# Steps 5 to 45 of a segment recurrence: K and V row chunks shared by both feature halves, two more head blocks of Wo paired, and another filler table

## The chip, the cores and the metric

The kernel runs on one core of a Trainium2 chip. The metric is the device time of one execution in microseconds, as the median of several runs. A NeuronCore has the engines PE (TensorE: matmuls, and PEld, its weight loads), DVE (VectorE), ACT (ScalarE), POOL (GpSimd) and SP (SyncE, which here issues DMAs). They run side by side and wait for one another by semaphores.

## The reference, cut to what matters

A layer of segment-recurrent attention with a memory of 8 rows, followed by a gated feed-forward layer. `x` is (1, 2048, 640), H = 32 heads of 128, segments of 32 rows, 64 segments one after the other:

```python
for s in range(n_seg):                       # 64 steps
    h = concat([mem, xs], axis=1)            # 8 memory rows + 32 rows of x
    q, k, v = h @ Wq, h @ Wk, h @ Wv         # 640 -> 32 heads x 128
    p = softmax(mask(q @ k.T * scale))
    o = (p @ v) @ Wo                         # 4096 -> 640
    mem = o[:, :M]                           # the next step's memory
    outs.append(o[:, M:])
h  = x + attention(layernorm(x))
h2 = h + ffn(layernorm(h))
```

The next step's memory rows are this step's output, so the 64 steps can't run side by side.

## The kernel before, in words

All operations are put into one list by a Python class. Each names its engine and the tiles and PSUM banks that it reads and writes, and the class derives the waits between engines; each engine then runs its own operations in the order of the list. So the order of the Python calls is the order on each engine.

A step handles 32 rows at once: 8 rows of memory and 24 of x. The last 8 rows of each segment are done for four segments together, in passes that the steps run as extra work (`extra_units`, called by `filler`). An activation tile has 128 rows by 32 columns and is the stationary operand of a matmul; the weights W are streamed past it, 512 columns at a time. Four such matmuls go side by side in the four column groups of the array (g = 0 to 3). One such set of four is called a round here, and its four weight loads a round of loads.

`project` (L398) computes one of K (j = 1), Q (j = 0) or V (j = 2) for a feature half (i = 0 or 1, 2048 features each) from five row chunks c of 128 rows, added up in one PSUM bank: five rounds for each half, so 30 rounds a step for K, Q and V. Half 0 of K and V goes to bank P2, half 1 to P3; Q uses P0 and P1. Every round loads its chunk of the activation. `held=True` leaves out the first load, where the same chunk was used just before (`again`, L390, a matmul without a load; `WAYS` runs half 1 through the chunks backwards so that this fits). `parts` cuts a 512-column matmul into two of 256, each with a load of its own.

The table `FILL` and `fill_of` say for each step how many such extra instructions are put in: loads that could have been held, and split matmuls. With them four steps issue 3072 PE instructions.

A step's order on PE, by the calls in the loop: K (half 0 in chunks 0 to 2, which need only the first part of the new memory, key "m"; then chunks 3 and 4, key "m2"; then half 1), the previous step's value product (`pv_x`, L712), Q, V half 0 in chunks 0 to 3, scores of half 0 (`scores`, L515) in two parts around chunk 4, V half 1 in the same way around the scores of half 1, the memory rows' products (`pv_mem`, L569) with `filler` work between them, and Wo.

After each half of K and Q, ACT copies the bank to SBUF (`to_tok`, L443) and DVE transposes it (`flip`, L438). The halves of V are copied by ACT alone (`to_v`, L443, tile Vp). `pv_mem(s, 0)` needs Vp's half 0 and the masked exponents Pbd from DVE.

Wo is done in two passes, each over 16 head blocks. `wo_split` (L634) takes eight pairs of head blocks, with 320 columns and four matmuls to a pair, into bank P1. `wo_pass` (L617) takes the other 16 blocks one by one, with 160 columns and four matmuls to a block, into P3. `fold_split` folds P1 to the sum SA: two DVE transposes (L647), two ACT copies (L650), and one addition, on POOL in three of four steps and on DVE in the steps with s % 4 = 1 (L652). `to_act_split` transposes P3 on DVE (L661) and adds SA (L663) into the next step's activation, in two parts (m and m2). `rows_split` then reads P3 (L668) and P1 (L670) for the output rows. Extra work (`filler(2)`) stands on PE between Wo and the next step's K.

Of the kernel before, what the change touches and what calls it, by code (L numbers as in the profile page):

```python
# [27 lines left out]
class _Graph:  # L28
# [149 lines left out]
def build_kernel(nc, A_x, A_mem0, A_Wq, A_Wk, A_Wv, A_Wo, A_seg_len, B_W_gate, B_W_up, B_W_down, out):  # L178
    _, S, D = A_x.shape
    M = A_mem0.shape[1]  # L180
    _, H, Dh = A_Wq.shape
# [97 lines left out]
    def bank(b):  # L279
        return ps[:, b * 512:(b + 1) * 512]  # L280
# [19 lines left out]
    def B(n):  # L300
        return ("B", n)
# [96 lines left out]
    def project(act, akeys, j, halves, banks, chunks=range(5), ends=(0, DC - 1), held=False, parts=0):  # L398
        swap = 1 if j == 2 and akeys[0][0] == "acte" else 0

        def f(pe):
            left = parts
            for c in chunks:
                for n, i in enumerate(halves):
                    for g in range(4):
                        o = 2048 * i
                        w = (W[:, j, c, o + 512 * (g ^ swap):o + 512 * (g ^ swap) + 512] if j == 2 else
                             W[:, j, c, o:o + 2048].rearrange("p (h e) -> p h e", e=128)[:, :, 32 * g:32 * g + 32])
                        a = (bank(banks[n])[32 * g:32 * g + 32, :], act[:, c, :], w)
                        if n == 0 and not (held and c == chunks[0]):  # L410
                            k = min(left, 2) if c != ends[0] else 0
                            left -= k
                            for q in range(2 if k else 1):
                                b = a if not k else (a[0][:, 256 * q:256 * q + 256], a[1],
                                                     w[:, 256 * q:256 * q + 256] if j == 2 else w[:, 8 * q:8 * q + 8])
                                if q and k == 1:
                                    ins = again(pe, *b, c == ends[0], c == ends[1], g)
                                else:
                                    ins = pe.matmul(*b, start=(c == ends[0]), stop=(c == ends[1]), skip_group_check=True)  # L419
# [181 lines left out]
    def oT_keys(p, hf):  # L601
        return [("oT", p, n, hf) for n in "mx"]
# [3 lines left out]
        add("pool", lambda g: g.tensor_copy(oTe[:, :, o:o + M], oT[p][:, :, 32:40]),  # L606
            r=[("oT", p, "x", kh) for kh in range(2)], w=[("oTe", s % 4)])

    def wo_pass(p, bk, halves=(0, 1), groups=range(4)):
        src = oT[p]  # L610
        for hf in halves:
            for lo, hi in [(4 * g, 4 * g + 4) for g in groups]:
                def f(pe, hf=hf, lo=lo, hi=hi):
                    for hb in CH[16 * hf + lo:16 * hf + hi]:
                        w = Wo[:, hb, :].rearrange("p (c g j) -> p g c j", g=4, j=32)
                        for gg in range(4):
                            i = pe.matmul(bank(bk)[32 * gg:32 * gg + 32, 0:160], src[:, hb, 0:32], w[:, gg],  # L617
                                          start=(hb == CH[16 * halves[0]]), stop=(hb == CH[-1]), skip_group_check=True)
                    return i
                add("pe", f, r=oT_keys(p, hf) + [("Wo", hf, lo // 4)], w=[B(bk)])  # L620

    def wo_split(p, bk):
        for g in range(4):
            wo_pairs(p, bk, g)

    def wo_pairs(p, bk, group):
        src = oT[p]

        def f(pe):
            for n in (2 * group, 2 * group + 1):  # L630
                for q in range(4):
                    hb = CH[2 * n + q // 2]
                    w = ap(Wo, hb * D + 32 * q, [[64 - 128 * (q // 2), 2], [128, DC], [1, 32]])
                    i = pe.matmul(bank(bk)[32 * q:32 * q + 32, 0:320], src[:, hb, 0:32], w, start=(n == 0),  # L634
                                  stop=(n == 7), skip_group_check=True)
# [525 lines left out]
    row_moments(xl, ("xl",), n_rows(1))  # L1161

    WAYS = ((range(DC), (0, DC - 1)), (range(DC - 1, -1, -1), (DC - 1, 0)))
    FILL = (56, 39, 7, 52)

    def fill_of(s):
        n = {1: 0, 2: 0, 3: 0, 4: 27, 52: 40, 56: 40, 50: 0, 51: 25, 54: 0, 55: 25, 57: 39, 58: 0, 59: 27, 60: 40, 61: 39, 62: 50, 63: 0}.get(s, FILL[s % 4])
        alone = min(n // 4, 3)
        rest = n - 4 * alone
        return [k < 3 - alone for k in range(3)], [2 * ((rest // 2 + k) // 4) + (k == 0 and rest % 2) for k in range(4)]  # L1170

    for s in range(1, NSEG):
        last = s == NSEG - 1
        par = s % 2
        nb = s // 4 + 1
        ln = 64 + 128 * nb < S
# [12 lines left out]
        if s > 0:  # L1189
# [19 lines left out]
                    dma(farv_d[:, 512 * i:512 * i + 512], tok[2 + i], r=tok_keys(2 + i), w=[("farv", i)])  # L1209
                dma(ends_d[:, :], ends[:, :], r=END_KEYS, w=[("ends",)])  # L1210
            for i in range(2):
                if i == 0:
                    soon = min(parts[0], 8 * (KC - 1))
                    project(a, [k for k in ks if k[-1] != "m2"], 1, (0,), (P2,), range(KC), parts=soon)
                    project(a, ks, 1, (0,), (P2,), range(KC, DC), parts=parts[0] - soon)
                else:
                    project(a, ks, 1, (1,), (P3,), *WAYS[1], held=held[0], parts=parts[1])
                to_tok((P2, P3)[i], i, "act")
                if last and i == 1:
                    load_piece(("Ko", 0), "act")  # L1220
                flip(i, Ko, i, [("Ko", i)])
# [36 lines left out]
            if last:  # L1258
                load_piece(("Vp", 0), "act")
# [13 lines left out]
        if last:  # L1273
# [303 lines left out]
```

## Time and profile before

| | us |
|---|---|
| median of 3 runs | 976.83 (975.82 to 977.68) |
| the profiled execution, its own time | 977.37 |
| its span, first to last instruction | 975.4 |
| granted TensorE clock, mean | 1.00 |

How to read what follows: L12 is line 12 of the kernel. A line of the timeline gives the start in us from the span's start, the duration in us, the engine, the source line, the operation, what it writes and reads, the shape and a count of instructions merged into the line, and in brackets the engine's idle time just before with what ended it ("issue" where the profile shows nothing waited for). Starts of PE are the measure of its pace; the duration of a matmul runs from its start to its modelled end and overlaps with the next one's.

### The profile page before, as it was taken

Reading aid. Unit: us, or ns where it says so; the run is one execution under the profiler, and the core shown is the slowest. Engines: PE = TensorE matmul, PEld = TensorE weight load, DVE = VectorE, ACT = ScalarE, POOL = GpSimd, SP = SyncE. Lnnn points to the kernel's source line nnn. Section 1 sums busy time; section 2 is a strip of 40 time slices with the busy share of each in tenths; the row PEclk is TensorE's granted clock in tenths of the full one; section 3 lists DMA queues with packets and bytes.
Section 4 is the critical chain, followed back from the end, with each engine's and each line's share of the span. In section 5 each row is a group of like instructions: output and inputs, shape, how many; then the busy total and the mean of one; then the engine's idle time right before and its main releaser. Section 6 shows DMA issues by size and latency. Waiting matters only on the chain.

```text
span 975.4 us, 56715 instructions
## 1 busy us (share of the span) xinstructions
PE 952.1 (98%) x26144; PEld 536.0 (55%) x24915; DVE 726.6 (74%) x2041; ACT 522.6 (54%) x1326; POOL 185.7 (19%) x423
## 2 busy tenths in 40 slices
PE   4999999999999999999999999999999999999998
PEld 1345565655665656565656565566666665444444
DVE  3668888888888888888888888888888883445332
ACT  1476666666666666666666666655555552122121
POOL 7021212121313131313131313020201110000000
PEclk9999999999999999999999999999999999999999
DMA  9961212222232323232323322232424246714100
GB/s 363 416 229 47 44 47 43 55 52 56 59 80 61 76 61 76 64 77 66 79 62 78 65 63 55 43 96 71 128 74 117 69 125 212 278 21 95 28 14 28
DMA packets 97300, 91.95 MB, mean 94 GB/s; under 512 B 57674, under 2 KB 80658, under 8 KB 94994
## 3 DMA queue, kind: packets, MB, share of 16 engines
q1 hardware_dynamic: 95328, 87.36, 31.5%
q8 instruction: 201, 3.29, 1.4%
q10 hardware_dynamic: 1730, 0.96, 0.4%
q14 instruction: 41, 0.34, 0.1%
HBM read 50.75 MB, written 15.22 MB: 68 GB/s over the span
## 4 chain that ended last, share of the span: by engine, by line
PE 94%; SPq 3%; DMA 2%; issue 1%; POOL 0%; ACT 0%; DVE 0%; POOLq 0%
PE ps L419 47%; PE ps L1066 9%; PE ps L617 7%; PE ps L392 7%; PE ps L634 7%; PE ps L683 4%; PE ps L1390 3%; PE ps L918 3%; SPq L357 3%; PE ps L515 3%; PE ps L712 2%; DMA Wo<-in_A_Wo_dram 2%; PE ps L569 1%; PE ps L1079 0%; PE ps L1405 0%
## 5 line engine op out<-in xcount | busy, mean ns | idle before, releaser
L419 PE MATMUL ps<-W,act_r 128*32 128x512 bf16 (+1 forms) x8335 | 466.4, 360 | 0.6 <-ACT tok L443 0.4
L419 PEld LDWEIGHTS ps<-W,act_r 128*32 128x32 bf16 x8335 | 218.9, 96 | 166.0 <-issue 22.4
L443 ACT ACTIVATE tok<-ps 128x512 bf16<-128x512 f32 x184 | 106.3, 594 | 60.9 <-PE ps L419 48.1
L443 ACT ACTIVATE tox<-ps 128x512 bf16<-128x512 f32 x138 | 81.8, 598 | 59.3 <-PE ps L419 48.9
L438 DVE STREAM_TRANSPOSE Ko<-tox 128x512 bf16<-128x512 bf16 x128 | 89.0, 696 | 29.3 <-ACT tox L443 28.6
L419 PE MATMUL ps<-W,act_e 128*32 128x512 bf16 x1008 | 97.3, 383 | 3.5 <-DVE TBf L496 2.0
L597 DVE STREAM_TRANSPOSE oT<-tox 128x512 bf16<-128x512 bf16 x128 | 94.8, 741 | 0.0
L438 DVE STREAM_TRANSPOSE Qo<-tok 128x512 bf16<-128x512 bf16 x124 | 85.5, 689 | 0.9 <-ACT tok L443 0.2
L617 PE MATMUL ps<-Wo,oT 128*32 128x160 bf16 x4032 | 82.0, 233 | 1.2 <-DMA Wo<-in_A_Wo_dram 1.0
L634 PE MATMUL ps<-Wo,oT 128*32 128x320 bf16 x2016 | 80.0, 299 | 0.4 <-DVE oT L591 0.4
L617 PEld LDWEIGHTS ps<-Wo,oT 128*32 128x32 bf16 x4032 | 70.5, 97 | 11.7 <-DVE oT L591 2.7
L443 ACT ACTIVATE Vp<-ps 128x512 bf16<-128x512 f32 x127 | 75.2, 592 | 0.5 <-ACT Vp L443 0.5
L392 PE MATMUL ps<-W,act_e 128*32 128x512 bf16 x712 | 70.5, 385 | 0.0
L1094 ACT ACTIVATE g<-ps 128x512 bf16<-128x512 f32 x43 | 25.0, 593 | 77.1 <-PE ps L1066 75.6
L650 ACT ACTIVATE SA<-TA 64x40 f32<-64x40 f32 x126 | 29.6, 235 | 65.3 <-DVE TA L647 64.5
L531 ACT ACTIVATE Pm<-ps 128x64 bf16<-128x64 f32 x126 | 28.1, 223 | 67.3 <-PE ps L515 66.1
L591 DVE STREAM_TRANSPOSE oT<-om 128x128 bf16<-128x128 bf16 x126 | 39.2, 311 | 31.1 <-ACT om L583 31.0
L515 PE MATMUL ps<-Qo,Ko 128*32 128x40 bf16 x2048 | 61.5, 181 | 0.0
L634 PEld LDWEIGHTS ps<-Wo,oT 128*32 128x32 bf16 x2016 | 51.1, 96 | 18.0 <-DVE rm L581 0.8
L515 PEld LDWEIGHTS ps<-Qo,Ko 128*32 128x32 bf16 x2048 | 46.8, 94 | 25.2 <-DVE Qo L438 17.7
L1095 DVE TENSOR_TENSOR hT<-g,ps 128x512 bf16<-128x512 bf16 x43 | 29.6, 688 | 40.1 <-PE ps L1066 35.5
L523 POOL COPY Qo<-ends 128x256 bf16<-128x256 bf16 x32 | 14.0, 438 | 238.2 <-DVE oT L591 231.2
(155 smaller groups left out, 1532.0 us busy)
## 6 DMA issues: line engine op xcount, KB each, us to landing
VM<-Vp SPq DMA_DIRECT2D x126, 65.0 KB
VM<-Vp SPq DMA_DIRECT2D x63, 130.0 KB
W<-in_A_Wk_dram SPq DMA_DIRECT2D x5, 1024.0 KB
W<-in_A_Wq_dram SPq DMA_DIRECT2D x5, 1024.0 KB
W<-in_A_Wv_dram SPq DMA_DIRECT2D x5, 1024.0 KB
Wo<-in_A_Wo_dram SPq DMA_DIRECT2D x8, 640.0 KB
attn_d<-wtok SPq DMA_DIRECT2D x248, 7.5 KB
xt<-in_A_x_dram SPq DMA_DIRECT2D x16, 160.0 KB
```

The source lines that it names most:

```text
L392: return pe.add_instruction(mybir.InstMatmult(name=nc.get_next_instruction_name(), engine=mybir.EngineType.PE, ins=[pe.lower_ap(rhs), pe.l ...
L419: ins = pe.matmul(*b, start=(c == ends[0]), stop=(c == ends[1]), skip_group_check=True)
L438: add("dve", lambda v: v.transpose(dst[:, 16 * i:16 * i + 16, 0:32], tok[t][:, :].rearrange("p (h f) -> p h f", f=32)), r=tok_keys(t), w=keys)
L443: add("act", lambda a: a.activation(dst, src, ACTF.Copy), r=r, w=w)
L515: i = pe.matmul(bank((P0, P1)[hf])[q:q + 32, o:o + 40], (Ko if a == 0 else Ke[p])[:, h, :], Qo[:, h, :], start=True, stop=True, skip_group ...
L591: add("dve", lambda v: v.transpose(ap(oT[par], 160 * hf, [[40, 4], [320, 4], [1, 8]]), ap(om, 128 * hf, [[1, 4], [4, 32]])), r=[("om", hf) ...
L597: add("dve", lambda v, kh=kh: v.transpose(ap(oT[p], 160 * kh + M, [[320, 4], [40, 4], [1, 32]]), ap(tox, 128 * kh, [[256, 4], [1, 4], [4, ...
L617: i = pe.matmul(bank(bk)[32 * gg:32 * gg + 32, 0:160], src[:, hb, 0:32], w[:, gg], start=(hb == CH[16 * halves[0]]), stop=(hb == CH[-1]), ...
L634: i = pe.matmul(bank(bk)[32 * q:32 * q + 32, 0:320], src[:, hb, 0:32], w, start=(n == 0), stop=(n == 7), skip_group_check=True)
L650: add("act", lambda a, lo=lo, to=to: a.activation(SA[to:to + 64], TA[lo:lo + 64, 1, :, 0:M], ACTF.Copy), r=[("TA", 1)], w=[("SA", to)])
L683: ins = pe.matmul(bank(bk)[32 * q:32 * q + 32, 0:320], src[:, hb, 0:32], w[:, 2 * (q % 2):2 * (q % 2) + 2], start=(i == 0), stop=(i == 15) ...
L1066: ins = pe.matmul(bank(bk), w[:, c, lo:lo + 128], xn2T[par][:, c, :], start=(c == 0), stop=(c == DC - 1))
```

## The change

`rounds` is new. It issues single rounds for a list of (chunk, half) pairs and loads a chunk only where it differs from the pair before, so that two neighbouring rounds on the same chunk, one for each half, share their loads. In steps 5 to 45 (`woven`):

- K runs as (0,0) (1,0) (2,0), (2,1), (3,0) (3,1) (4,0), then the copy of half 0, then (4,1) (1,1) (0,1). Half 1 begins at the fourth round, with the first keys ("m") alone.
- V runs as (0,0) (0,1) (1,0) (1,1), the scores around chunk 4 of half 0, then (2,0) (3,0), which end half 0 at chunk 3, then (3,1) (2,1), and the scores of half 1 around chunk 4 of half 1. ACT's copy of half 0 stays where it was in ACT's order, behind the exponent of the first scores.
- In steps with s % 4 other than 1, `wo_split` takes a ninth pair, the first two blocks of the second pass, and `wo_pass` skips them. The ninth pair needs the second half of oT.
- `FILL` becomes (0, 0, 2, 0); steps 3 and 4 get 60 filler instructions each; steps 46, 47 and 49 keep their old numbers by name, and step 48 gets 50 for 56.

```diff
+    def rounds(act, akeys, j, seq, ends, held=False):
+
+        def f(pe):
+            before = seq[0][0] if held else None
+            for c, i in seq:
+                for g in range(4):
+                    o = 2048 * i
+                    w = (W[:, j, c, o + 512 * g:o + 512 * g + 512] if j == 2 else
+                         W[:, j, c, o:o + 2048].rearrange("p (h e) -> p h e", e=128)[:, :, 32 * g:32 * g + 32])
+                    a = (bank((P2, P3)[i])[32 * g:32 * g + 32, :], act[:, c, :], w)
+                    start, stop = c == ends[i][0], c == ends[i][1]
+                    if c == before:
+                        ins = again(pe, *a, start, stop, g)
+                    else:
+                        ins = pe.matmul(*a, start=start, stop=stop, skip_group_check=True)
+                before = c
+            return ins
+        add("pe", f, r=list(akeys) + [("W", j, c) for c, _ in seq], w=[B((P2, P3)[i]) for i in sorted({i for _, i in seq})] + [("Wdone", j)])
+
...
-    def wo_pass(p, bk, halves=(0, 1), groups=range(4)):
+    def wo_pass(p, bk, halves=(0, 1), groups=range(4), skip=0):
...
-            for lo, hi in [(4 * g, 4 * g + 4) for g in groups]:
+            for lo, hi in [(max(4 * g, skip), 4 * g + 4) for g in groups]:
...
-    def wo_split(p, bk):
-        for g in range(4):
-            wo_pairs(p, bk, g)
-
-    def wo_pairs(p, bk, group):
+    def wo_split(p, bk, more=False):
+        for g in range(4 + more):
+            wo_pairs(p, bk, g, 7 + more)
+
+    def wo_pairs(p, bk, group, end=7):
...
-        add("pe", f, r=oT_keys(p, 0) + [("Wo", 0, group)], w=[B(bk)])
+        add("pe", f, r=oT_keys(p, group // 4) + [("Wo", group // 4, group % 4)], w=[B(bk)])
...
-    FILL = (56, 39, 7, 52)
+    FILL = (0, 0, 2, 0)
...
-        n = {1: 0, 2: 0, 3: 0, 4: 27, 52: 40, 56: 40, 50: 0, 51: 25, 54: 0, 55: 25, 57: 39, 58: 0, 59: 27, 60: 40, 61: 39, 62: 50, 63: 0}.get(s, FILL[s % 4])
+        n = {1: 0, 2: 0, 3: 60, 4: 60, 46: 7, 47: 52, 48: 50, 49: 39, 50: 0, 51: 25, 52: 40, 53: 39, 54: 0, 55: 25, 56: 40, 57: 39, 58: 0, 59: 27, 60: 40, 61: 39, 62: 50, 63: 0}.get(s, FILL[s % 4])
...
+        woven = 4 < s < 46
...
-                if i == 0:
+                if woven:
+                    first = [k for k in ks if k[-1] != "m2"]
+                    for keys, seq, hold in (((first, ((0, 0), (1, 0), (2, 0)), False), (first, ((2, 1),), True),
+                                             (ks, ((3, 0), (3, 1), (4, 0)), False)), ((ks, ((4, 1), (1, 1), (0, 1)), True),))[i]:
+                        rounds(a, keys, 1, seq, ((0, 4), (2, 0)), hold)
+                elif i == 0:
...
-            project(a, ks, 2, (0,), (P2,), range(4), held=not last and held[2])
+            VE = ((0, 3), (0, 4))
+            if not woven:
+                project(a, ks, 2, (0,), (P2,), range(4), held=not last and held[2])
+            else:
+                rounds(a, ks, 2, ((0, 0), (0, 1), (1, 0), (1, 1)), VE, held[2])
             scores(s, 0, (0, 1))
-            project(a, ks, 2, (0,), (P2,), (4,))
+            project(a, ks, 2, (0,), (P2,), (4,), ends=(0, 3 if woven else 4))
             scores(s, 0, (2, 3))
             if not last:
                 exp_mem(s, 0)
                 first_exp = G.ops[-1]
                 mask_mem(s, 0)
+                if woven:
+                    rounds(a, ks, 2, ((2, 0), (3, 0)), VE)
             to_v(P2, Vp, 0, ("Vp",), "act")
...
-        project(a, ks, 2, (1,), (P3,), range(4))
+        if woven:
+            rounds(a, ks, 2, ((3, 1), (2, 1)), VE, True)
+        else:
+            project(a, ks, 2, (1,), (P3,), range(4))
...
-        wo_split(par, P1)
+        more_pairs = s % 4 != 1 and woven
+        wo_split(par, P1, more_pairs)
...
-        wo_pass(par, P3, (1,))
+        wo_pass(par, P3, (1,), skip=2 * more_pairs)
```

More of the change, by code (lines that the diff above doesn't have):

```diff
@@ L617, in f @@
                             i = pe.matmul(bank(bk)[32 * gg:32 * gg + 32, 0:160], src[:, hb, 0:32], w[:, gg],
-                                          start=(hb == CH[16 * halves[0]]), stop=(hb == CH[-1]), skip_group_check=True)
+                                          start=(hb == CH[16 * halves[0] + skip]), stop=(hb == CH[-1]), skip_group_check=True)
                     return i
                 add("pe", f, r=oT_keys(p, hf) + [("Wo", hf, lo // 4)], w=[B(bk)])
-    def wo_split(p, bk):
-        for g in range(4):
-            wo_pairs(p, bk, g)
-    def wo_pairs(p, bk, group):
+    def wo_split(p, bk, more=False):
+        for g in range(4 + more):
+            wo_pairs(p, bk, g, 7 + more)
+    def wo_pairs(p, bk, group, end=7):
         src = oT[p]
         def f(pe):
-            for n in (2 * group, 2 * group + 1):
+            for n in range(2 * group, min(2 * group + 2, end + 1)):
                 for q in range(4):
@@ L634, in f @@
                     i = pe.matmul(bank(bk)[32 * q:32 * q + 32, 0:320], src[:, hb, 0:32], w, start=(n == 0),
-                                  stop=(n == 7), skip_group_check=True)
+                                  stop=(n == end), skip_group_check=True)
             return i
-        add("pe", f, r=oT_keys(p, 0) + [("Wo", 0, group)], w=[B(bk)])
+        add("pe", f, r=oT_keys(p, group // 4) + [("Wo", group // 4, group % 4)], w=[B(bk)])
     flat = "p c j -> p (c j)"
```

## The prediction

> **What bounds the kernel now.** I read the page first (busy times, DMA queues, chain of waits), then busy times by stretch with one step of the loop to a stretch, then the timeline of single steps.
>
> ```profile
> span 975.4 us, 56715 instructions
> PE 952.1 (98%) x26144; PEld 536.0 (55%) x24915; DVE 726.6 (74%) x2041; ACT 522.6 (54%) x1326; POOL 185.7 (19%) x423
> ...
> q8 instruction: 201, 3.29, 1.4%
> ...
> PE 94%; SPq 3%; DMA 2%; issue 1%; POOL 0%; ACT 0%; DVE 0%; POOLq 0%
> ```
>
> TensorE's matmuls are 94% of the chain that ended last. Queue q8 carries instruction text: 201 blocks for 26144 + 24915 instructions, some 254 to a block, so a four-step cycle of 3072 is 12 blocks and one of 2816 is 11.
>
> ```profile
> 59.70:71.62 11.92, 11.92 (x372) 6.21 (x340) 10.05 (x32) 8.00 (x21) 5.36 (x11) 1.00 0.33 99
> ...
> 238.90:251.60 12.70, 12.47 (x391) 7.83 (x370) 10.25 (x31) 7.51 (x19) 2.52 (x4) 1.00 0.45 77
> ...
> 407.08:419.03 11.95, 11.95 (x384) 6.83 (x360) 10.42 (x31) 8.01 (x21) 3.61 (x4) 1.00 0.36 81
> 419.03:430.96 11.93, 11.93 (x392) 7.31 (x373) 10.23 (x30) 7.50 (x19) 1.10 (x3) 1.00 0.34 87
> ...
> 442.91:454.92 12.01, 12.01 (x404) 7.53 (x395) 10.38 (x33) 7.35 (x20) 5.41 (x11) 1.00 0.16 42
> ```
>
> Columns: stretch, its length, then PE and weight loads (PEld), DVE, ACT, POOL busy with their counts, granted clock, DMA share, GB/s. A step runs from one start of the previous step's value product to the next. Steps 30 to 33, from 407.08 to 454.92, take 47.84 us, with PE busy throughout at the full clock. Step 1, which has no filler loads, takes 11.92 with 340 loads; step 31 takes 11.93 with 373. So filler costs about 0.01 a step, and little is left to win. Step 16 (238.90) is the one long step, 0.77 over step 31.
>
> Now the timeline of step 31, from the scores to the memory product:
>
> ```profile
> 422.42 0.19 PE L515 MATMUL ps<-Qo,Ko 128*32 128x40 bf16 x4
> ...
> 422.45 0.19 PE L515 MATMUL ps<-Qo,ends 128*32 128x40 bf16 x4
> ...
> 422.84 1.03 PE L419 MATMUL ps<-W,act_r 128*32 128x512 bf16 x16
> 422.89 0.67 DVE L438 STREAM_TRANSPOSE Qo<-tok 128x512 bf16<-128x512 bf16 x1
> 423.10 0.22 ACT L531 ACTIVATE Pm<-ps 128x64 bf16<-128x64 f32 x1 [0.49 <-PE ps L515]
> 423.21 0.59 ACT L443 ACTIVATE Vp<-ps 128x512 bf16<-128x512 f32 x1
> ...
> 423.61 0.10 PEld L515 LDWEIGHTS ps<-Qo,Ko 128*32 128x32 bf16 x4 [0.23 <-DVE Qo L438]
> 423.70 0.19 PE L515 MATMUL ps<-Qo,Ko 128*32 128x40 bf16 x4
> ...
> 424.10 0.10 PEld L569 LDWEIGHTS ps<-ends,Pbd 128*32 128x32 bf16 x4
> 424.12 0.23 PE L569 MATMUL ps<-ends,Pbd 128*32 128x129 bf16 x4
> ...
> 424.23 0.39 PE L419 MATMUL ps<-W,act_e 128*32 128x512 bf16 x4
> ...
> 424.44 0.39 PE L392 MATMUL ps<-W,act_e 128*32 128x512 bf16 x4
> ...
> 424.66 0.39 PE L419 MATMUL ps<-W,act_e 128*32 128x512 bf16 x4
> ```
>
> A round of four 512-column matmuls takes 0.215 us (424.23 to 424.66 are two). L392 is the round without its own loads: 0.22 after it, 0.21 after a round with loads. **Weight loads lie wholly under the matmuls here.** Also: four rounds run from 422.84 to 423.70, and the query transpose, done at 423.56, is answered by PE at 423.61, 0.05 later.
>
> **The change part by part.** All figures are for the 41 steps 5 to 45.
>
> *Fewer loads and pieces.* A four-step cycle loses 256 instructions: 80 loads by sharing row chunks (a step's K loads go from 36 to 28, V's from 36 to 24), 24 instructions by Wo pairing (8 more and 16 fewer in three of the steps), and 152 of filler (the table's 154 less 2). The 512-column rounds stay 30 a step for K, Q and V. Loads are hidden by the rounds, so they are worth nothing; were that cover gone, each would cost what it now hides. Split pieces and shorter Wo rounds have small fixed costs. Step 1 against steps 31 and 30 bounds this between 0.01 and 0.03 a step; I take 0.012, nearest to step 31, because step 30's excess reads as a wait of PE for the query transpose: the one quoted above leaves no more than 0.09 of room: **-0.5 us**. The other end is -1.2. The filler added to steps 3 and 4 costs 0.03 in all by the same price. Wo itself streams as much as before: one 320-column round for two of 160.
>
> *The value half 0 is finished later.* Before, its five rounds ended ahead of the second score pair, and ACT copied it from 423.21, done 423.80. After, chunks 2 and 3 of that half come behind both score pairs: at 422.84 and 423.06. The last ends at 423.06 + 0.38 + 0.01 for its fourth matmul = 423.45. ACT starts a hand-over later (0.06, the row of L661 below), at 423.51, and needs 0.59: 424.10. Then PE must hear of it:
>
> ```profile
> 47.76 0.37 ACT L583 ACTIVATE om<-ps,rm 128x128 bf16<-128x128 f32 x1 [1.48 <-DVE rm L581]
> ...
> 48.19 0.09 PEld L634 LDWEIGHTS ps<-Wo,oT 128*32 128x32 bf16 x1 [0.78 <-DVE rm L581]
> ```
>
> That load had to wait for ACT to leave its bank: 48.13 to 48.19, 0.06. So the memory product's loads start at 424.16 instead of 424.10. Its place in PE's order is unchanged, since nine rounds and three score pairs stand ahead of it both times. Bounds: 0.04, if PE answers as it answered the transpose (0.05) and the last digits fall well; 0.10, if it were as slow as DVE answering POOL in step 26 below (0.10). I take 0.05, nearest to this row: 41 x 0.05 = 2.05. Where PE now waits some 0.02 for the scores (I put that at a third of the steps, from 11.95 against 11.93), the new wait swallows that: -0.25. **Net +1.8 us**, between +1.4 and +3.9. Behind it on PE stand filler, the second memory product and all of Wo; DVE's reciprocals wait for them, so everything moves along and nothing is made up. The value DMAs wait for the other half's copy, which stays in place, so SP's queue is passed by nothing.
>
> *The ninth Wo pair.* In three of four steps the split pass is a round longer.
>
> ```profile
> 425.64 1.26 PE L634 MATMUL ps<-Wo,oT 128*32 128x320 bf16 x32
> ...
> 426.72 1.28 PE L617 MATMUL ps<-Wo,oT 128*32 128x160 bf16 x64
> ...
> 426.95 0.58 DVE L647 STREAM_TRANSPOSE TA<-ps 128x160 f32<-128x160 f32 x2
> ...
> 427.33 0.48 ACT L650 ACTIVATE SA<-TA 64x40 f32<-64x40 f32 x2 [1.06 <-DVE TA L647]
> ...
> 427.95 0.27 POOL L652 TENSOR_TENSOR SA<-SA,TA 128x40 f32<-128x40 f32 x1 [0.30 <-ACT SA L650]
> ...
> 428.06 0.28 DVE L661 STREAM_TRANSPOSE TBf<-ps 128x96 f32<-128x96 f32 x1 [0.53 <-PE ps L617]
> ...
> 428.38 0.18 DVE L663 TENSOR_TENSOR act_r<-TBf,SA 128x24 bf16<-128x24 f32 x1
> ...
> 428.61 0.84 PEld L419 LDWEIGHTS ps<-W,act_r 128*32 128x32 bf16 x25 [0.46 <-DVE act_r L663]
> 428.69 1.04 PE L419 MATMUL ps<-W,act_r 128*32 128x512 bf16 x21
> ...
> 428.85 0.32 DVE L668 TENSOR_TENSOR fold<-ps,fold 128x160 f32<-128x160 f32 x1
> ```
>
> Its eight rounds take 425.64 to 426.72, 0.135 each, so its sums start 0.14 later. Today POOL's sum ends at 428.22 and DVE's transpose at 428.34, so the sum has cover. Later by 0.14 it ends at 428.36. What DVE then does, step 26 shows, where POOL was late by chance:
>
> ```profile
> 368.29 0.27 POOL L652 TENSOR_TENSOR SA<-SA,TA 128x40 f32<-128x40 f32 x1 [0.18 <-POOL oTe L606]
> ...
> 368.66 0.18 DVE L663 TENSOR_TENSOR act_r<-TBf,SA 128x24 bf16<-128x24 f32 x1
> ...
> 368.90 0.45 PEld L419 LDWEIGHTS ps<-W,act_r 128*32 128x32 bf16 x16 [0.52 <-DVE act_r L663]
> 368.92 0.61 PE L419 MATMUL ps<-W,act_r 128*32 128x512 bf16 x12
> ```
>
> POOL ended at 368.56, DVE began 0.10 later, and the load came 0.24 after DVE's start, 0.02 ahead of its matmul. So: 428.36 + 0.10 + 0.24 = 428.70 against a matmul now at 428.69. Late by 0.01 to 0.03; I take 0.02 in 30 steps: **+0.6 us**, between 0 and 0.9.
>
> *Key half 1 starts at the fourth round*, in the bank that L668 reads. L668 ends at 429.17 today, 0.08 later with the sum above: 429.25, heard at 429.31. The fourth round is due at 428.71 + 0.65 = 429.36. The cover is 0.05; gone by 0.05 it would cost 2 us more, and it cannot gain. I take 0.1 for a step in which DVE is late. The key copies come 0.65 apart instead of 1.08; ACT needs 0.59 for each, so the second is as early as today.
>
> *Instruction blocks.* Step 16's excess is PE without instructions:
>
> ```profile
> 243.73 0.81 PE L419 MATMUL ps<-W,act_r 128*32 128x512 bf16 x9 [0.23 <-issue]
> ```
>
> The new spacing may miss that moment or meet another; I put it at 0, from -0.8 to a rival below.
>
> **The sum:** -0.5 + 0.03 + 1.8 + 0.6 + 0.1 = **+2.0 us**. On the profiled execution's own 977.37 (975.4 of span) that is 979.4, or 978.6 if step 16's 0.77 does not come back. The profiled execution is 0.54 above the median of 976.83, about what such a stall accounts for, so I set the sum on the median: **978.9**.
>
> **The rivals.**
>
> *Both waits are hidden* (the copy and the sum come 0.05 and 0.02 sooner than I read them). Then -0.5 alone: 976.3, and 975.6 without a stall like step 16's. For it: the margins are of the size of the rows' last digit. Against: all rows give the same sign.
>
> *Loads do cost time, so it is faster.* Of the 256 instructions some 187 are loads (80 shared, 12 of Wo, 40 fillers, 55 of pieces), 47 rounds of four. A score round with its four loads takes 0.03 us (422.42 to 422.45); at that price ten cycles give 14 us: 963. It decides if a round without loads is shorter than one with them; 424.23 to 424.66 speak against. The Trainium skill, TensorE: Matmul & The Clock Gate, section Back-to-back issue gap, says that in a stream of load and matmul pairs both set the spacing, and its section on LDWEIGHTS gives columns over 1.2 as the nanoseconds, by my estimate 27 ns for 32 columns, 13 us here; the L392 rows disagree.
>
> *Blocks arrive too late, much slower.* Eleven blocks a cycle no longer lie alike in each step. From 423.61 to 426.72 PE uses some 210 instructions, 240 in the steps that carry the extra end pass: a block's worth in 3.1 us. If a block's fetch is slower than that, PE stands still; at half of step 16's 0.77 in each of ten cycles, 3.9 us more: 982.8. Against: one stall in 41 steps today. The Trainium skill, Runtime: NRT & Kernel Launch, section Instruction fetch mechanics, calls the crossing of a 256-instruction block mostly hidden; step 16 shows the exception.
>
> *The change does not cut the count*: not plausible, the loops spell it out; 0.01, 976.8.
>
> **How the numbers follow.** A measurement of this kernel tells about 0.2% (1.95 us) from no change. Forecast 0.50, of which 0.36 lies above 978.8 and 0.14 within. Both hidden 0.24 (0.21 same, 0.03 faster). Loads or fewer blocks pay 0.09, faster. Blocks too late 0.16, slower. So slower 0.52, same 0.36, faster 0.12. The forecast's own range is 977.6 to 980.8; the whole goes from the hidden case, 975.6, to 982.0, short of the block case's 982.8.
>
> **What would show it.** In the changed profile: the memory product's loads wait for ACT's value copy, with 0.05 of idle PE in each step of 5 to 45; key loads wait for DVE with PE idle 0.02, except in every fourth step; a step of 11.98 to 12.00 instead of 11.93; 10 fewer blocks; rounds still 0.215 apart. I am wrong if steps come out at 11.92, if rounds without loads get shorter, or if idle PE is put down to issue.

## The result, and the profile after

The changed kernel takes 986.84 us (median of 6 runs, 984.25 to 989.69); before, beside it, 977.41 (975.82 to 979.66). The ratio is 1.0096, with a 95% interval of 1.0082 to 1.0111: 9.4 us slower, where +2.0 was forecast.

The page of after (span and instructions, busy times, the instruction queue, the chain of waits):

```profile
span 987.9 us, 54194 instructions
PE 960.8 (97%) x25488; PEld 496.7 (50%) x23050; DVE 725.8 (73%) x2041; ACT 527.3 (53%) x1326; POOL 186.2 (19%) x423
...
q8 instruction: 191, 3.13, 1.3%
...
PE 91%; SPq 4%; DMA 3%; DVE 1%; issue 1%; POOL 0%; ACT 0%; POOLq 0%; DVEq 0%
```

TensorE has 656 matmuls and 1865 loads fewer, and 10 blocks of instructions fewer. Yet its busy time is up by 8.7 us, and its share of the chain is down from 94% to 91%. This execution took 989.69, 2.85 above the median, and 1.9 us of that lie in step 2 (13.80 long, 11.92 before), which the change does not touch: VectorE waited there for input rows.

```profile
73.82 0.89 DVE L361 BATCH_NORM_STATS2 st<-xl 128x6 f32<-128x320 bf16 x2 [2.56 <-DMA xl<-in_A_x_dram]
```

Now the busy times by stretch, with steps 1 to 4, 5 to 45 and 46 to 62 as stretches. Before:

```profile
59.70:107.41 47.71, 47.71 (x1491) 25.85 (x1390) 39.70 (x117) 31.02 (x80) 11.30 (x21) 1.00 0.26 63
107.41:598.37 490.96, 490.73 (x15946) 295.23 (x15357) 420.53 (x1227) 309.56 (x804) 121.24 (x226) 1.00 0.27 63
598.37:802.24 203.87, 203.87 (x6540) 124.55 (x6421) 167.31 (x489) 122.11 (x316) 31.32 (x71) 1.00 0.33 87
```

After, the same three, and then steps 19, 30, 31 and 35 by themselves:

```profile
60.76:110.98 50.22, 48.61 (x1524) 26.85 (x1424) 39.28 (x116) 30.86 (x80) 11.33 (x21) 1.00 0.23 66
110.98:608.54 497.56, 496.25 (x15247) 254.20 (x13458) 420.17 (x1227) 314.32 (x805) 121.43 (x226) 1.00 0.26 62
608.54:814.28 205.74, 204.66 (x6533) 124.71 (x6416) 167.16 (x488) 122.19 (x316) 31.44 (x71) 1.00 0.32 86
...
280.31:293.70 13.39, 12.29 (x369) 6.30 (x317) 10.27 (x29) 7.63 (x20) 1.10 (x3) 1.00 0.29 76
414.40:426.46 12.06, 12.06 (x369) 5.89 (x317) 10.32 (x30) 8.11 (x22) 3.62 (x4) 1.00 0.37 83
426.46:438.52 12.06, 12.06 (x368) 5.86 (x317) 10.21 (x29) 7.63 (x20) 1.10 (x3) 1.00 0.31 82
475.15:487.53 12.38, 12.29 (x369) 6.32 (x318) 10.28 (x29) 7.64 (x20) 1.11 (x3) 1.00 0.31 80
```

There are two losses. Every step of the loop is longer: step 31 takes 12.06 instead of 11.93. And some steps have a stop besides (19: 13.39, 35: 12.38), inside the loop and behind it, where the code is the old one.

To keep the two apart I call a step **undisturbed** if it has no stop, and take for each of the four kinds of step (its number modulo 4) the third shortest of the loop. Over the 41 steps that makes 489.8 us before and 494.9 after: +5.0. The rest of the loop is stops: 1.1 before (0.77 of it step 16), 2.7 after.

**The longer step** is the memory product's wait. The timeline of step 31, from the end of value half 0 to the memory product (compare the rows of step 31 before, where the score row at 423.70 is followed by the product at 424.12):

```profile
430.27 0.60 PE L439 MATMUL ps<-W,act_r 128*32 128x512 bf16 x8
...
430.52 0.22 ACT L550 ACTIVATE Pm<-ps 128x64 bf16<-128x64 f32 x1 [0.48 <-PE ps L534]
...
430.92 0.60 ACT L462 ACTIVATE Vp<-ps 128x512 bf16<-128x512 f32 x1 [0.17 <-PE ps L439]
...
431.13 0.19 PE L534 MATMUL ps<-Qo,Ko 128*32 128x40 bf16 x4
...
431.63 0.13 PEld L588 LDWEIGHTS ps<-ends,Pbd 128*32 128x32 bf16 x4
431.67 0.24 PE L588 MATMUL ps<-ends,Pbd 128*32 128x129 bf16 x4
```

From the score row to the product it is 0.54 now, 0.42 before. ScalarE's copy ends at 430.92 + 0.60 = 431.52 and the load comes at 431.63, **0.11 later**; I had taken 0.06. It is so in all 41 steps: at least 0.113, and 0.114 at the median. The wait can't be found as idle time: matmul ends are modelled, the last score matmul's lies behind the product's start, and so the step shows 12.06 of busy PE in 12.06. Only the starts of two equal rows, set side by side, show it.

**A stop**, that of step 19, on the timeline:

```profile
288.25 1.01 PE L636 MATMUL ps<-Wo,oT 128*32 128x160 bf16 x46
...
290.36 0.39 PE L636 MATMUL ps<-Wo,oT 128*32 128x160 bf16 x10 [1.10 <-issue]
```

In the midst of one Wo pass, which waits for nothing else, TensorE stands for 1.10 us. The DMA view says where the next block of instructions was. In step 31, which has no stop, a block is read between 6.04 and 7.04 us after the step's start (432.50 to 433.50); in step 19 that stretch (286.35 to 287.35) has no packet on any queue, and the block is read in the stretch from 7.19 us on (287.50 to 288.50). These are the lines on q8 of the first and the last:

```profile
q8 instruction: 1, 0.02, 5.5%
```

```profile
q8 instruction: 1, 0.02, 8.5%
```

By the packets' own starts it is read 7.24 us into step 19 and 6.07 into step 31. What held it up for these 1.2 us is not in the trace.

### The profile page after: what moved, and what is told of

Read it like the earlier page. It is cut to its first block, busy times and chain, and to the rows that moved or that the text cites. A ratio compares the mean times of both kernels' runs of the same rounds, so it can differ in the third digit from the quotient of the medians.

```text
span 987.9 us, 54194 instructions
## 1 busy us (share of the span) xinstructions
PE 960.8 (97%) x25488; PEld 496.7 (50%) x23050; DVE 725.8 (73%) x2041; ACT 527.3 (53%) x1326; POOL 186.2 (19%) x423
## 4 chain that ended last, share of the span: by engine, by line
PE 91%; SPq 4%; DMA 3%; DVE 1%; issue 1%; POOL 0%; ACT 0%; POOLq 0%; DVEq 0%
PE ps L419 28%; PE ps L392 13%; PE ps L439 10%; PE ps L1085 9%; PE ps L653 7%; PE ps L636 7%; PE ps L702 4%; SPq L357 4%; PE ps L1425 3%; PE ps L937 3%; PE ps L534 2%; PE ps L731 2%; DMA Wo<-in_A_Wo_dram 2%; PE ps L588 2%; DMA at<-xl 0%
## 5 line engine op out<-in xcount | busy, mean ns | idle before, releaser
L419 PE MATMUL ps<-W,act_r 128*32 128x512 bf16 (+1 forms) x4786 | 300.7, 369 | 0.5 <-ACT tok L462 0.4
L419 PEld LDWEIGHTS ps<-W,act_r 128*32 128x32 bf16 x4786 | 123.3, 96 | 110.1 <-issue 29.3
L439 PE MATMUL ps<-W,act_r 128*32 128x512 bf16 x1804 | 148.3, 379 | 0.0
L392 PE MATMUL ps<-W,act_r 128*32 128x512 bf16 x1528 | 144.4, 380 | 0.1
L419 PE MATMUL ps<-W,act_e 128*32 128x512 bf16 x1008 | 100.0, 384 | 4.1 <-DVE TBf L515 2.0
L439 PEld LDWEIGHTS ps<-W,act_r 128*32 128x32 bf16 x1804 | 43.8, 96 | 99.7 <-issue 74.7
L616 DVE STREAM_TRANSPOSE oT<-tox 128x512 bf16<-128x512 bf16 x128 | 91.3, 713 | 0.0
L653 PE MATMUL ps<-Wo,oT 128*32 128x320 bf16 x2136 | 85.3, 299 | 1.0 <-issue 0.6
L636 PE MATMUL ps<-Wo,oT 128*32 128x160 bf16 x3792 | 78.9, 233 | 2.0 <-issue 1.1
L636 PEld LDWEIGHTS ps<-Wo,oT 128*32 128x32 bf16 x3792 | 69.5, 97 | 9.5 <-DVE oT L610 2.4
L392 PE MATMUL ps<-W,act_e 128*32 128x512 bf16 x712 | 72.8, 385 | 0.0
L653 PEld LDWEIGHTS ps<-Wo,oT 128*32 128x32 bf16 x2136 | 57.6, 96 | 19.0 <-issue 2.2
```

Source lines behind the costliest of these rows:

```text
L392: return pe.add_instruction(mybir.InstMatmult(name=nc.get_next_instruction_name(), engine=mybir.EngineType.PE, ins=[pe.lower_ap(rhs), pe.l ...
L439: ins = pe.matmul(*a, start=start, stop=stop, skip_group_check=True)
L616: add("dve", lambda v, kh=kh: v.transpose(ap(oT[p], 160 * kh + M, [[320, 4], [40, 4], [1, 32]]), ap(tox, 128 * kh, [[256, 4], [1, 4], [4, ...
```

## The experiments

Two theories to begin with. **A**: the new wait for the value copy costs the 5.0 of the undisturbed steps. **C**: the 11 blocks of a cycle lie badly, and that makes the stops. Rivals stand with the expectations. All ratios are to the kernel before on the same chip; "loop" is steps 5 to 45 of the one profiled execution, "undisturbed" as above.

| kernel | instructions a cycle | us (median) | ratio, 95% interval | loop | undisturbed | rest |
|---|---|---|---|---|---|---|
| before | 3072 | 977.41 | 1 | 490.96 | 489.8 | 1.1 |
| after | 2816 | 986.84 | 1.0096 (1.0082 to 1.0111) | 497.56 | 494.9 | 2.7 |
| e1_swap | 2816 | 980.60 | 1.0022 (1.0010 to 1.0035) | 492.20 | 491.3 | 0.9 |
| e2_early | 2816 | 987.25 | 1.0094 (1.0073 to 1.0116) | 500.37 | 494.9 | 5.4 |
| e3_even | 3072 | 982.84 | 1.0043 (1.0028 to 1.0059) | 495.84 | 495.6 | 0.3 |
| e4_bare | 2918 | 985.95 | 1.0070 (1.0048 to 1.0092) | 498.46 | 489.3 | 9.1 |
| e5_even_swap | 3072 | 978.39 | 1.0019 (1.0008 to 1.0030) | 492.21 | 491.9 | 0.3 |
| e6_sooner | 3072 | 977.51 | 1.0004 (0.9994 to 1.0015) | 491.01 | 490.4 | 0.6 |
| e7_sooner_no_pair | 3072 | 976.94 | 1.0002 (0.9989 to 1.0015) | 490.70 | 490.2 | 0.5 |
| e8_shift | 3072 | 997.97 | 1.0220 (1.0202 to 1.0238) | 506.86 | in no cycle | |
| e9_after_less_32 | 2816 | 985.09 | 1.0085 (1.0058 to 1.0113) | 496.61 | 494.8 | 1.8 |
| e10_before_plus_48 | 3072 | 979.60 | 1.0029 (1.0011 to 1.0047) | 492.03 | 489.9 | 2.2 |
| e11_before_plus_160 | 3072 | 984.97 | 1.0098 (1.0063 to 1.0133) | 499.59 | 489.9 | 9.7 |

The kernel before beside e1 to e4 had a median of 978.16, beside e5 to e8 976.92, beside e9 to e11 977.05; so the ratios are compared, not the times.

### The wait taken in another order

The first memory product needs VectorE's mask and ScalarE's copy. Its two waits are written one after the other; the edit turns them round, in steps 5 to 45.

```
-            for d in op.waits:
+            for d in op.waits[::-1] if op.turn else op.waits:
...
-            add("pe", f, r=[("Pbd", a, hf) ...
+            op = add("pe", f, r=[("Pbd", a, hf) ...
+            op.turn = hf == 0 and 4 < s < 46
```

> The changed kernel, with the two waits of the first memory product's loads in steps 5 to 45 taken in the other order: VectorE's first, ScalarE's second. Same instructions, same count. Theory A (the new wait is for ScalarE's value copy, and it costs 0.116 a step rather than the forecast 0.05 because ScalarE's signal is heard by a separate wait instruction 0.04 after the copy's end, which takes 0.05 more, and the load stands behind it): with ScalarE's signal heard by the load itself, the load comes 0.06 to 0.07 after the copy's end instead of 0.114, the score-to-memory-product stretch shrinks from 0.217 to about 0.17, and 41 steps give 2.0 us back: about 984.9. Rival B (TensorE answers ScalarE this slowly whoever carries the wait, or the copy isn't what it waits for): the stretch stays at 0.217 and the time at 986.8.

Ratio 1.0022: by the ratios 7.2 of the 9.4 us are gone, where 2.0 were expected. Step 31 of this kernel on the timeline:

```profile
424.07 0.60 ACT L463 ACTIVATE Vp<-ps 128x512 bf16<-128x512 f32 x1 [0.17 <-PE ps L440]
...
424.28 0.19 PE L535 MATMUL ps<-Qo,Ko 128*32 128x40 bf16 x4
...
424.72 0.10 PEld L589 LDWEIGHTS ps<-ends,Pbd 128*32 128x32 bf16 x4
424.72 0.24 PE L589 MATMUL ps<-ends,Pbd 128*32 128x129 bf16 x4
```

The copy ends at 424.67 and the load comes 0.05 later (0.051 at the median of the 41 steps), about as I had forecast for the change itself; score row to product is 0.44. So theory A stands, and the doubled size comes from the order of two waits. The undisturbed steps give 3.6 of the gain (494.9 to 491.3), more than 2.0, because the product's matmul now starts with its load and not 0.03 behind it. The rest lies in fewer stops. Only the order of the two waits tells this kernel from after, so the order took these stops away too. By what path isn't shown; it fits that the block which came late in step 19 is read 6.07 to 7.24 us into the loop's steps 3 modulo 4 in after, and 5.53 to 6.46 here.

### Value half 0 ahead of half 1

```
-rounds(a, ks, 2, ((0, 0), (0, 1), (1, 0), (1, 1)), VE, held[2])
+rounds(a, ks, 2, ((0, 0), (0, 1), (1, 0), (1, 1), (2, 0)), VE, held[2])
...
-rounds(a, ks, 2, ((2, 0), (3, 0)), VE)
+rounds(a, ks, 2, ((3, 0),), VE)
```

> The changed kernel, with value half 0 finished one round earlier: five of its and half 1's rounds ahead of the first score pair instead of four, one behind the second pair instead of two. Same loads, same count, same sums. Theory A (the memory product waits for the copy of this half): the copy's rounds end 0.215 earlier, but the scores' exponential, which ScalarE does first, comes 0.215 later and the copy can start some 0.1 after that exponential's start; so it ends about 0.07 earlier and the wait falls from 0.11 to 0.02 to 0.04: 41 steps give 2.9 to 3.7 us back, about 983.5. Rival B (the exponential holds the copy back wholly, or the mask for the memory product becomes the later one): the stretch stays at 0.2 and the time at 986.8.

Nothing changed, 1.0094, and the fault is in the edit: seven rounds stand ahead of half 0's end either way, so it only puts the scores a round later. It still excludes something. In its step 32, which begins at 437.37, ScalarE does:

```profile
441.64 0.22 ACT L550 ACTIVATE Pm<-ps 128x64 bf16<-128x64 f32 x1 [0.71 <-PE ps L534]
441.82 0.60 ACT L462 ACTIVATE Vp<-ps 128x512 bf16<-128x512 f32 x1
```

The exponential starts 4.27 into the step instead of 4.06 (430.52, step begun at 426.46), the copy at 4.45 as before (4.46). So the exponential didn't set the copy's start; the last round of the half does.

### As many instructions as before

Filler (split pieces, repeated loads) in the key and query rounds of the changed kernel, so that each cycle has 3072 instructions again and each step outside the loop its old count.

```
-    FILL = (0, 0, 2, 0)
+    FILL = (84, 59, 35, 80)
...
-    n = {1: 0, 2: 0, 3: 60, 4: 60, 46: 7, 47: 52, 48: 50, ...
+    n = {1: 0, 2: 0, 3: 0, 4: 27, 46: 7, 47: 52, 48: 56, ...
```

> The changed kernel, filled up with split pieces and repeated loads in the key and query rounds, so that each four-step cycle has 3072 instructions as before (12 blocks of 256) and every step outside the loop has its old count. The value-copy wait and the Wo pairs stay. Theory C (the 11 blocks of a cycle lie unevenly, one boundary falls where a wait has held TensorE's sequencer back and dense Wo work follows, so that a block fetched a little late stops TensorE): the stops put down to issue in steps 3, 19, 33 to 35, 45, 53 and 58 go, worth 3 to 5 us, and the filler costs 0.4 to 1.0: 982.3 to 984.3, with less spread between executions. Rival D (the stops come from transfers at their own moments, whatever the spacing): as many stops, 987 to 988.

1.0043: **256 more instructions a cycle make it 0.5% faster**. The loop:

```profile
107.67:603.51 495.84, 495.78 (x16390) 294.03 (x14910) 421.26 (x1227) 314.35 (x805) 121.31 (x226) 1.00 0.27 62
603.51:807.40 203.89, 203.56 (x6538) 123.51 (x6420) 167.05 (x489) 122.20 (x316) 31.37 (x71) 1.00 0.33 87
```

The undisturbed steps are 0.7 longer (the filler's price), the stops of the loop are down to 0.3, and steps 46 to 62 are back at 203.9. Theory C stands against D.

### The kernel before without its filler

```
-    FILL = (56, 39, 7, 52)
+    FILL = (0, 0, 0, 0)
```

> The kernel before, with its filler table at zero: 2918 instructions a cycle in place of 3072 (11.4 blocks), nothing else. Theory C (uneven blocks cost time by themselves): the step itself is 0.01 shorter (0.5 us in all), but idle time put down to issue appears at block boundaries, 2 to 4 us: 979 to 981. Rival D (spacing doesn't matter, and filler is only work): 976.5 to 977.3, with no more stops than before's one.

1.0070: nothing of the woven order is in this kernel, and it is 7 us slower than before. Its steps 23 and 27 and its loop by stretch, and the stop of step 27 on the timeline:

```profile
328.18:340.10 11.92, 11.92 (x372) 6.21 (x340) 10.22 (x30) 7.51 (x19) 1.10 (x3) 1.00 0.32 84
376.45:390.54 14.09, 12.50 (x373) 7.41 (x342) 10.22 (x30) 7.51 (x19) 1.10 (x3) 1.00 0.31 76
...
109.87:608.33 498.46, 494.18 (x15357) 276.06 (x14381) 418.83 (x1227) 309.70 (x804) 121.22 (x226) 1.00 0.27 62
```

```profile
385.19 0.62 PE L617 MATMUL ps<-Wo,oT 128*32 128x160 bf16 x24
387.40 0.40 PE L419 MATMUL ps<-W,act_e 128*32 128x512 bf16 x4 [1.59 <-issue]
```

An undisturbed step takes 11.92, so dropping the filler and its loads is worth 0.5 in 41 steps (489.8 to 489.3). The stops cost 9.1, more than either theory had expected. This execution took 988.24, 2.3 above the median; by the ratio the stops of a usual one cost some 7.

### Both mends, and a half 0 that is really sooner

e5 is e3 with e1's order of waits:

> Both mends together: the changed kernel with the two waits of the first memory product in the other order, and with each cycle filled up to 3072 instructions. If the wait (theory A) and the uneven blocks (theory C) are two separate causes, the undisturbed step of the even kernel (12.08) falls by the 0.09 that the other order of waits gave by itself, 41 x 0.09 = 3.7 under 982.8: 979.1, with no more than one stop in the loop. If the other order only helped because it let the blocks come earlier (rival), nothing is left to gain once they lie evenly: 982 to 983.

1.0019; the undisturbed sum falls from 495.6 to 491.9, 3.7 as expected. So in the undisturbed steps the gain of the other order stands beside the filler's price, whatever the count: the wait is a cause by itself.

The stops don't add up like that. Take from each ratio what the undisturbed steps gained or lost: over before, after has 4.4 us left for stops, e1 0.7, e3 and e5 none (-1.5 and -0.3), each known to some 1.5. With the old order of waits, the count of 2816 costs 5.2 us (1.0096 against 1.0043); with the new one it costs 0.3 (1.0022 against 1.0019). The stops of after came of both together, and either edit takes nearly all of them away.

e6 is e3 with one round of half 1 moved behind half 0's end, and four instructions of filler a step fewer, since four loads are added:

```
-rounds(a, ks, 2, ((0, 0), (0, 1), (1, 0), (1, 1)), VE, held[2])
+rounds(a, ks, 2, ((0, 0), (0, 1), (1, 0), (2, 0)), VE, held[2])
...
-rounds(a, ks, 2, ((2, 0), (3, 0)), VE)
+rounds(a, ks, 2, ((3, 0),), VE)
...
-rounds(a, ks, 2, ((3, 1), (2, 1)), VE, True)
+rounds(a, ks, 2, ((3, 1), (2, 1), (1, 1)), VE, True)
```

> The even kernel with value half 0 truly finished a round sooner: one round of half 1 (chunk 1) is moved behind its end, at the price of four loads a step; the filler is four instructions a step shorter, so the counts stay. The waits keep their order. Theory A: the copy ends 0.215 sooner, the memory product waits for nothing (stretch 0.10 as before instead of 0.217), the step falls from 12.08 to about 11.965, and 41 steps give 4.7 back: 978.1. Rival (ScalarE starts the copy no sooner, because of its exponential): the stretch stays near 0.2 and the time near 982.8.

1.0004, level with before. Step 31:

```profile
424.72 0.60 ACT L472 ACTIVATE Vp<-ps 128x512 bf16<-128x512 f32 x1
...
425.14 0.19 PE L544 MATMUL ps<-Qo,Ko 128*32 128x40 bf16 x4
...
425.56 0.23 PE L598 MATMUL ps<-ends,Pbd 128*32 128x129 bf16 x4
```

The copy ends at 425.32, the product comes at 425.56, and score row to product is 0.42, as before the change. The undisturbed sum is 490.4: the wait cost 5.2 us there.

e7 is e6 without the ninth Wo pair, its eight instructions a step given back by the filler:

```
-        more_pairs = s % 4 != 1 and woven
+        more_pairs = False
```

> The same kernel without the ninth Wo pair (eight instructions a step more of Wo, eight fewer of filler in three steps of four). What is left of the change is the shared row chunks and the earlier start of key half 1. If the ninth pair delays the sum and so the next step's keys (theory: 0.01 in the stretch ahead of the keys and 0.01 in the keys), the step falls by about 0.02 in three of four steps, 0.6 in all: 977.5, level with before. If the late key start has another reason, such as key half 1 at the fourth round: the stretches ahead of and in the keys stay at 0.875 and 2.28.

1.0002. The undisturbed sum falls by 0.2 and not 0.6: ahead of the keys the stretch goes from 0.865 to 0.871 back to 0.863, but steps 2 modulo 4 wait 0.01 for the queries instead.

### Where the blocks begin

Three kernels that differ from before only in the filler of steps 3 and 4, so that in all later steps the block boundaries fall 48, 96 or 160 instructions earlier in the step; the cycle stays at 3072, 12 blocks that lie alike in every cycle. Theory C has two readings here: C1, what counts is that the blocks lie evenly; C2, what counts is where in a step the boundaries fall. In the expectations, boundaries "further on" are these same ones: they move on in number, and so come earlier in the step.

```
-        n = {1: 0, 2: 0, 3: 0, 4: 27, ...
+        n = {1: 0, 2: 0, 3: 12, 4: 63, ...      (48)
+        n = {1: 0, 2: 0, 3: 60, 4: 63, ...      (96)
+        n = {1: 0, 2: 0, 3: 98, 4: 89, ...      (160)
```

> The kernel before with 48 more instructions of filler in steps 3 and 4, the boundaries 48 instructions on, half of the shift that cost 20 us. Theory C2: between before and that, some 980 to 990, with idle time of TensorE put down to issue in the end pass of Wo of every fourth step or in the key rounds after it, as there. Rival (that loss was a matter of one place only, which 48 does not reach): 977 to 978.

> The kernel before, with 96 more instructions of filler in steps 3 and 4 and nothing else: each cycle still has 3072 instructions, so blocks lie alike in each step, but their boundaries fall 96 instructions further on from step 5 to the end. Theory C1 (what counts is that blocks lie evenly): as before, 977.5 to 978.5. Theory C2 (what counts is where in a step the boundaries fall): stops put down to issue come back in many steps, 980 or more.

> The kernel before with 160 more instructions of filler in steps 3 and 4, the boundaries 160 instructions on, which is also 96 short of the old place. Theory C2: the cost isn't in proportion to the shift but follows the places; the boundaries come past the score and memory product stretch, so 978 to 990 with the stops in other lines than with 96. Rival (any shift away from the tuned place costs the more the further it goes): over 998.

Ratios 1.0029, 1.0220 and 1.0098: +2.8, +21 and +9.6 us, most of it in steps that hold the same instructions as before. C1 falls: that the blocks lie alike in every cycle isn't enough; where they begin decides, and not in proportion to the shift. The 979.60 of the shift by 48 is just short of the 980 that C2 asked for, and above the 978 of its rival. The loop of e8, its steps 29 and 31, and the stop of step 29:

```profile
107.43:614.29 506.86, 499.26 (x15944) 315.52 (x15355) 421.77 (x1227) 309.53 (x804) 121.22 (x226) 1.00 0.24 61
...
404.17:417.40 13.23, 12.28 (x402) 8.09 (x395) 10.33 (x33) 7.35 (x20) 5.41 (x11) 1.00 0.14 38
429.77:441.91 12.14, 12.14 (x393) 7.37 (x374) 10.38 (x30) 7.51 (x19) 1.10 (x3) 1.00 0.31 83
```

```profile
412.94 0.98 PE L683 MATMUL ps<-Wo,oTe 128*32 128x320 bf16 x22
414.87 0.45 PE L683 MATMUL ps<-Wo,oTe 128*32 128x320 bf16 x6 [0.95 <-issue]
```

With 96 the stops come in the end pass of Wo (L683) and in the first key rounds, with 160 nearly all in the second Wo pass (L617). The loop of e11:

```profile
109.46:609.05 499.59, 493.71 (x15945) 303.14 (x15356) 420.82 (x1227) 309.47 (x804) 121.08 (x226) 1.00 0.27 62
```

Its undisturbed steps are those of before (489.9), all the rest is stops; this execution took 990.94, 6.0 above the median.

That it is block boundaries can be counted. Number TensorE's records (loads, matmuls, its separate waits) through each trace, and take from 80 to 812 us the places where two matmuls start 0.45 us or more apart: 53 in the profiled executions of before, after, e2, e4, e8 and e11. In 50 of them the matmul that comes late has nearly the same number modulo 256, 191 to 194; over all thirteen traces it is 58 of 63.

The instruction queue shows what TensorE waits for at these places. Count blocks and packets in order, with a boundary at the number 193 modulo 256: in 2308 crossings between 80 and 812 us, none comes sooner than 2.16 us after its block's packet starts, and in the 58 stops TensorE goes on 2.18 to 3.14 us after it. The packet itself starts 0.77 us (median) behind the boundary ahead of it where there is no such stop, and 1.9 where there is one; in step 19 of after it was 2.2. So a stop is a block that is read late, met by 256 instructions that are soon used up (3.6 us at the median, without the stop, against 4.1). Why the packet starts late at some places, the traces don't show.

> The changed kernel with 32 instructions of filler fewer in step 4: from step 5 on each block boundary falls 32 instructions later in the step, still 11 blocks a cycle; nothing in the steps 5 to 45 themselves changes. Theory C2 (the place of the boundaries in the step sets the stops): the undisturbed steps stay at 12.06 to 12.10, and the stops of the loop move to other places or change in number, so the time leaves 986.8 by over 1.5 us, to either side. Theory C1 (11 uneven blocks cost the same wherever they begin): 985.5 to 988.

The changed kernel with 32 instructions of filler fewer in step 4 (`4: 60` becomes `4: 28`) has 1.0085. Its 985.09 is 1.75 below 986.8, just what C2 asked for; by the ratio it is 985.7 beside after's own before, what C1 said, and the intervals overlap. Undisturbed steps stay at 494.8, steps 46 to 62 are free of stops (203.46), and the loop has 1.8. This run doesn't tell the two apart; e8, e10 and e11 do.

## Why the prediction was wrong

**The value half 0** (+1.8, with bounds of 1.4 and 3.9). Mechanism and place were right: the product waits for ScalarE's copy in every step of the loop. The term was mis-sized: 0.115 more from score row to product instead of 0.05, which is 4.7 in 41 steps, and 5.2 by e6. The step that failed is "then PE must hear of it": I took the 0.06 of one row (the Wo load at 48.19) for any load that waits for ScalarE. This load waits for two engines, and while VectorE's wait is carried by the load and ScalarE's stands ahead of it as an instruction by itself, it is 0.11 from copy to load; with the two turned round it is the 0.05 of the forecast (e1). The row that I took has a separate wait too, but for ScalarE and a transfer together, and its record in the trace runs from 46.64 to 48.16: it ends 0.04 behind ScalarE, and the load follows 0.03 later. In step 31 of after the wait is for ScalarE alone; its record begins 0.04 behind the copy (431.56) and takes 0.05, as all 260 TensorE waits for one semaphore in that trace do, and the load follows 0.03 later. That 0.05 is what my row did not hold. Whether it is waiting for two at once that spares it, no run here tests. My upper bound of 0.10, from rows of yet other places, was too low by the same fault.

**Instruction blocks** (put at 0) was the step that failed outright. I saw that the excess of step 16 was PE without instructions, that a block is 256 and that 11 blocks would no longer lie alike, and then set the chance of stops at 0.16 because there was one stop in 41 steps. But that one stop is what the old spacing left over: with the filler away it is 9 us of them (e4), with the boundaries 96 earlier in the step it is 21 (e8). Of the 9.4 us, 5.0 lie in the undisturbed steps and 4.4 in stops. One way to undo them: 5.2 go when the count is put back (1.0096 to 1.0043), net of the filler's 0.7; 3.8 go with the wait (to 1.0004; 5.2 by the undisturbed steps) and 0.2 with the pair (to 1.0002), so that by the ratios the whole is accounted for within their intervals. But 7.2 go with the order of waits alone (e1), so the shares depend on what is undone first. The rival *blocks arrive too late* had the mechanism; its price of 3.9 was near, and it would have had to stand beside the wait, which helped to make the stops, and not in its place. The Trainium skill, Runtime: NRT & Kernel Launch, section Instruction fetch mechanics, calls the crossing of a block mostly hidden; that holds for the places where before has its boundaries, and not for those of e8.

**Fewer loads and pieces** (-0.5): right in size, 0.5 in e4's undisturbed steps. *Loads do cost time* falls: the loop of after has 1452 loads and 1143 matmuls fewer than that of e3, and its undisturbed steps are 0.7 us shorter in all.

**The ninth Wo pair** (+0.6, 0 to 0.9): right. The key loads waited for VectorE in these steps before too, but for less long: 0.46 us on average, and 0.52 now (lists of waits: total, times, longest; before's from 107 to 598 us, then after's).

```profile
PEld ps L419 <- DVE act_r L663: 13.8, 30, 0.5
```

```profile
PEld ps L439 <- DVE act_r L682: 16.1, 31, 0.5
```

In step 31 of after the sum ends and the keys start just as worked out (POOL's end at 435.91, VectorE 0.10 later, the load 0.24 after that):

```profile
435.64 0.27 POOL L671 TENSOR_TENSOR SA<-SA,TA 128x40 f32<-128x40 f32 x1 [0.43 <-ACT SA L669]
...
436.01 0.18 DVE L682 TENSOR_TENSOR act_r<-TBf,SA 128x24 bf16<-128x24 f32 x1
...
436.25 0.34 PEld L439 LDWEIGHTS ps<-W,act_r 128*32 128x32 bf16 x12 [0.53 <-DVE act_r L682]
```

In before, the first key matmul came 0.32 behind the start of VectorE's addition (median of steps other than 1 modulo 4), so there was room; now it comes 0.24 behind it, with its load, and in e7 0.32 again. The stretch ahead of the keys is longer by 0.010 to 0.017 in those steps, 0.4 in 30, and without the pair 0.2 comes back (e7).

**Key half 1 at the fourth round** (+0.1): no stop of its own; in e7, which keeps it, the keys take 2.27 as before.

*Both waits are hidden* was wrong: neither is. Of the signs I named, the steps of 12.06 in place of 11.98 to 12.00 and the idle PE put down to issue show where the forecast fails.

No version here beats before by more than the measurement tells. The best, e7, is level; what is left to win is the 0.5 of e4's undisturbed steps, and only with the blocks in good places.

## What to carry to other kernels

Where an instruction waits for two engines, let the instruction itself carry the wait that ends last, and put a hand-over's bounds wider than rows of other places say. In a kernel bound by one engine's instruction stream, look at undisturbed steps and at stops separately: a changed count moves every later block boundary, a late wait can bring stops as well as its own length (e1), and moving boundaries alone made the kernel before slower by 3 to 21 us. So try a change in count once at the old count, with filler, before its own worth is judged.

## What the runs showed of the hardware that was not expected

Taking 154 instructions a cycle out of the kernel before made it 0.7% slower, and putting 256 into the changed one made it 0.5% faster. A boundary of 256 instructions can fall so that nearly every cycle has a place where two matmuls start 0.5 to 1.25 us apart (e8), or so that one in ten cycles has (before), with every block still lying alike in each cycle. TensorE never went past a boundary sooner than 2.16 us after its block's packet had started. What delays a block's reading, by 1.2 us in step 19, stays open: no transfer was under way in the stretch where it was due.
